# The head of a fused attention and gated-FFN kernel in another order: two engines share its copies, and later loads change places

## The chip, the cores and the metric

One core of a Trainium2 chip runs one kernel. Its engines work at the same time, each through its own list of instructions in order: TensorE (PE in the profile; its weight loads are PEld), VectorE (DVE), ScalarE (ACT), GpSimd (POOL) and SyncE (SP). They wait for one another by semaphores. Data comes from the chip's memory by DMA, issued by an engine into a queue and moved by 16 DMA engines. The metric is the device time of one execution in microseconds; less is better. A verdict is faster or slower when the times differ by more than 2%.

## The reference

Eight batches, eight heads of 64. `x` has 512 rows per batch and head, `state` 32. Each reads the other by attention with a softmax; the two results are put one below the other (544 tokens per batch, 512 wide) and go through a gated feed-forward net of inner width 1536.

```python
scores  = scale * x @ state.T;   a  = softmax(scores);  xread = a  @ state     # (8, 8, 512, 64)
scores2 = scale * state @ x.T;   a2 = softmax(scores2); sread = a2 @ x         # (8, 8,  32, 64)
t = concatenate([xread, sread], axis=2)   # heads side by side: 4608 tokens x 512
gate = 1 / (1 + exp(-(t @ w_gate)));  val = t @ w_val                          # 512 -> 1536
out  = (gate * val) @ w_out                                                    # 1536 -> 512
```

## The kernel before

**What is computed per batch b.** `xT_mm`, `xT_cp`: x transposed by TensorE into PSUM and copied out (batches 0 and 1; later ones are transposed by a DMA that SyncE issues, `at_xT_dma`, L140). `S_mm`, `S_exp` (L147 to L167; for batch 0 in four pieces `Sq_mm`, `Sq_exp`, L174, L182): scores and their exponential E. `n_sum` (L208, L210; in pieces `nq_sum`, L186, L188): row sums and reciprocals on VectorE. `n_mul` (L227; `nq_mul`, L193): the normalised weights. `aT_mm`, `aT_cp` (L234, L244) or `aT_dma` (L248): these transposed. `at_Eb` (L200): four casts of E for the state's read, `rd_mm`, `rd_fin` (L265 to L275).

**The state is multiplied into the net's weights first.** `sw_visit(b, lo, n, ...)` (L286, L293) multiplies the state of batch b with columns lo to lo+n of both weights, head by head; `sw_cp` (L329) copies the result from PSUM to `SW`, in two halves e. So the attention's read and the first layer are one product: `gv_mm(b, f)` (L343) makes the gate and the value of the f-th 128 of the 1536 columns from `SW` and aT in four matmuls of 512 columns. `gv_th` (L364) is the tanh on ScalarE (the sigmoid is made of it), `gv_glu` (L369) the product on VectorE.

**The second layer** is a product of 2x2 blocks done with seven block products instead of eight. `ht_sum(t)` (L400) makes differences of blocks of `w_out` into T, `h_sum(t, half)` (L407) sums of blocks of the gated values into Sm; `h_mm(k, c)` (L442) is product k of batch 0, for one of two groups of rows; `w_keep` and `w_add` (L430, L433) put the products together, `w_store` sends the rows out.

**Loads.** `load_w(w, lo, n)` (L104) loads columns of the gate (w=0) or value (w=1) weights, `load_wo(q)` (L107) a third of `w_out`, `load_xh` and `load_x(2)` (L100, L82) x of batches 1 and 2, `load_sb(q)` (L527) the states of batches 2q and 2q+1. GpSimd issues all of these, one after the other among its other work, into one software queue (q0); they cast to bf16 where the target is bf16. `load_xp` is issued by SyncE, in hardware queue q1.

**What sets the order.** Nothing is reordered by a scheduler: each call emits its instructions at once, and each engine runs its own in the order of the calls in the source. Eight PSUM banks of one 128x512 tile each are named by hand (G0, G1, OU, S0 to S3, AT); a call that puts a new tile into a bank waits until the old one was read. The head, L560 to L838, is one list of calls written by hand that interleaves batch 0, batch 1 and the beginning of batch 2. Behind it stands a loop `step(b, f)` from b = 2 on, whose gate and value products are L355 and whose output products are L425.

Of the kernel before, what the change touches and what calls it, by code (L numbers as in the profile page):

```python
# [16 lines left out]
def kernel(  # L17
# [75 lines left out]
    def cast_xp(b, cp, lo, n):  # L93
        xh_tile(b)
        cp(xhs[b][:, lo:lo + n], xfs[b][:, lo:lo + n])

    def load_xh(b, lo, n):
        xh_tile(b)
        v = x[b].rearrange("h (p c) d -> p h c d", c=4)
        nc.gpsimd.dma_start(xhs[b][:, lo:lo + n], v[:, lo:lo + n])  # L100
# [9 lines left out]
    def zero(t, eng):  # L110
        (nc.gpsimd if eng is pool else nc.vector).memset(t, 0.0)
# [22 lines left out]
    def xT_cp(b, j, cp, n=1):  # L134
        cp(xT_tile(b)[:, j:j + n], held["xT", b, j])
# [192 lines left out]
    def sw_cp(b, lo, w, e, cp):  # L328
        cp(*sw_left.pop((b, lo, w, e)))  # L329
# [242 lines left out]
    cast_s(0, vec)
    cast_xp(0, act, 0, 2)
    load_xh(1, 4, 4)
    zero(sTd, vec)
    sT_mm(0, S1)
    load_xp(0, nc.sync, 4, 2)
    cast_xp(0, vec, 4, 2)
    xT_mm(0, 0, G1)
    load_xp(0, nc.sync, 2, 2)  # L580
    cast_xp(0, vec, 2, 2)
    xT_mm(0, 2, OU)
    xT_cp(0, 0, vec)
    xT_mm(0, 1, S3)
    sT_pad(0, act)
    sT_pad(1, act)
    xT_cp(0, 2, act)
    load_xp(0, nc.sync, 6, 2)
    cast_xp(0, act, 6, 2)
    Sq_mm(0, 2, S1)  # L590
# [24 lines left out]
    nq_mul(0, 0, pool)
    xT_mm(1, 2, S1, 2)
    nq_mul(0, 2, vec)
    nq_mul(0, 1, pool)
    xT_cp(1, 2, vec, 2)
    S_mm(1, 0, OU)  # L620
    S_exp(1, 0)
    load_w(1, 1280, 256)
# [1 line left out]
    at_Eb(0)
    aT_mm(0, AT)
    aT_cp(0, 0, act)
    S_mm(1, 1, S2)
    load_w(0, 1280, 256)
    aT_cp(0, 1, act)
    sw_visit(0, 256, 256, G0, G1)  # L630
    sw_cp(0, 256, 2, 0, vec)
# [26 lines left out]
    gv_mm(0, 2, S2, S1)
    gv_th(0, 2)
    gv_glu(0, 2)  # L660
    gv_mm(0, 9, AT, S3)
    gv_mm(1, 3, G1, S0)
# [8 lines left out]
    sT_mm(2, S1)
    gv_mm(1, 8, S2, S3)
    zero(sTz, pool)
    gv_th(1, 8)
# [25 lines left out]
    gv_mm(0, 10, G1, S3)  # L700
    sw_visit(0, 512, 512, OU, AT, 0)
    gv_glu(0, 8)
    gv_th(0, 10)
# [1 line left out]
    gv_glu(0, 0)
    gv_glu(0, 10)
    sw_cp(0, 512, 0, 0, act)
    gv_mm(0, 11, S2, G1)
    sw_visit(1, 512, 512, S3, S1, 0)
    sw_visit(0, 512, 512, OU, S0, 1)  # L710
    sw_cp(0, 512, 0, 1, vec)
    gv_th(0, 11)
    sw_visit(1, 512, 512, AT, G0, 1)
    sw_cp(1, 512, 0, 0, act)
    sw_cp(0, 512, 1, 1, act)
    gv_glu(0, 11)
    load_wo(1)
    sw_cp(0, 512, 1, 0, vec)
    rd_mm(1, S2)
    sw_cp(1, 512, 0, 1, act)  # L720
    gv_mm(0, 5, G1, OU)
    rd_fin(1)
    gv_th(0, 5)
    gv_mm(0, 7, S1, S3)
    sw_cp(1, 512, 1, 0, vec)
    sw_cp(1, 512, 1, 1, act)
    gv_glu(0, 5)
    nc.gpsimd.memset(xs[:, :, :, D:], 1.0)
    gv_mm(0, 4, S0, G0)
    gv_th(0, 7)  # L730
    gv_glu(0, 7)
    gv_th(0, 4)
    gv_glu(0, 4)
    gv_mm(0, 6, S1, G1)
    cast_x(2, pool, 4, 4)
    load_wo(2)
    gv_th(0, 6)
    sw_wide(2, 1, S3, OU, S0, G0, S2, AT)
    gv_glu(0, 6)
    sw_cp(2, 1, 0, 1, act)  # L740
# [6 lines left out]
    sw_cp(2, 1, 2, 0, act)
    h_sum(0, 1, vec)
    gv_mm(1, 6, OU, S3)
    sw_visit(1, 1280, 256, S1, G0)  # L750
# [4 lines left out]
    h_sum(2, 0, pool)
    h_sum(2, 1, vec)
    sw_cp(1, 1280, 2, 1, act)
    gv_mm(1, 4, G1, OU)
    gv_glu(1, 6)
    cast_x(2, pool, 0, 4)  # L760
    gv_mm(1, 7, S1, AT)
    gv_th(1, 4)
    sw_cp(1, 0, 2, 1, vec)
# [9 lines left out]
    h_mm(1, 0, AT)
    h_mm(1, 1)
    ht_sum(0, vec)
    h_sum(0, 0, pool)
    h_mm(5, 0, G1)
    S_mm(2, 0, OU)
    h_mm(5, 1)
    ht_sum(2, vec)  # L780
    h_sum(1, 0, vec)
    load_x(3, nc.sync)
    ht_sum(1, vec)
# [3 lines left out]
    sw_cp(1, 0, 2, 0, act)
    h_sum(3, 0, pool)
    w_keep('V1', 1)
    h_mm(6, 0)  # L790
    S_exp(2, 0)
    n_sum(2, 0)
    n_mul(2, 0, pool)
    S_mm(2, 1, G0)
    aT_dma(2, 0)
    S_exp(2, 1)
    gv_mm(1, 0, OU, S2)
    h_sum(3, 1, vec)
# [238 lines left out]
```

## Time and profile before

| | |
|---|---|
| time, median of 3 runs (lowest to highest) | 212.96 us (212.92 to 215.22) |
| profiled execution: time | 213.24 us |
| profiled execution: span | 211.5 us |
| instructions in the span | 5331 |
| mean granted TensorE clock | 0.992 |
| DMA packets, MB | 40920, 27.14 |

The span runs from the first to the last instruction that the profiler saw; 1.74 us of the execution lie around it. In the timelines a row gives the start and the length in us, the engine, the line and operation, what it writes and reads, how many instructions are taken together, and in brackets the idle time before them and who ended it. In the table of stretches the columns are PE, PEld, DVE, ACT and POOL busy time with their counts, then the granted clock, the DMA share and GB/s.

### The profile page before, as it was taken

The numbers are of one execution on the slowest core, as the hardware profiler recorded it, in microseconds if no ns is written. First come the engines' busy times: TensorE is split into PE (matmuls) and PEld (weight loads), VectorE is DVE, ScalarE is ACT, GpSimd is POOL, SyncE is SP. The second block draws the span as 40 slices with busy tenths as digits, with TensorE's granted clock in tenths as the row PEclk, the third lists the DMA queues.
The fourth block names the chain that finished last, engine by engine and source line by source line (L and its number), as shares of the span: only waits on it lengthen the run. The fifth ranks groups of instructions, "written<-read, shape, count | busy, mean of one in ns | idle before, by whom it ended". The sixth has DMA issues, their size and how long they took to land.

```text
span 211.5 us, 5331 instructions
## 1 busy us (share of the span) xinstructions
PE 204.5 (97%) x2089; PEld 133.4 (63%) x2089; DVE 160.7 (76%) x308; ACT 129.6 (61%) x244; POOL 78.7 (37%) x104
## 2 busy tenths in 40 slices
PE   7789999999999999999999999999999999999992
PEld 2555443677666666565656565657566666788982
DVE  2698899998987788578876887687848876864682
ACT  3878898754767477855786578647774673233210
POOL 8899467599042705900391029301500000000010
PEclk9799999999999999999999999999999999999999
DMA  6999999761689943985924621264110500130044
GB/s 190 181 192 192 213 289 192 115 215 38 78 219 342 132 94 133 289 73 160 295 58 48 186 87 28 56 101 175 26 34 1 201 2 0 76 126 0 4 171 126
DMA packets 40920, 27.14 MB, mean 128 GB/s; under 512 B 23616, under 2 KB 38720, under 8 KB 40896
## 3 DMA queue, kind: packets, MB, share of 16 engines
q1 hardware_dynamic: 30544, 19.47, 36.9%
q0 software_dynamic: 9920, 7.01, 20.5%
q10 hardware_dynamic: 432, 0.33, 0.7%
q8 instruction: 16, 0.26, 0.5%
q14 instruction: 8, 0.07, 0.1%
HBM read 18.35 MB, written 8.91 MB: 129 GB/s over the span
## 4 chain that ended last, share of the span: by engine, by line
PE 94%; DMA 2%; DVE 1%; ACT 1%; SPq 0%; issue 0%
PE gvp L355 30%; PE outp L425 29%; PE gvp L343 10%; PE gvp L358 5%; PE outp L442 4%; PE swp L286 4%; PE swp L293 2%; PE outp L484 2%; DMA xf<-in_x_dram 2%; PE Sp L147 1%; PE xTp L132 1%; PE outp L467 1%; PE rdp L262 1%; PE warm L517 1%; PE aTp L234 1%; PE rdp L265 1%
## 5 line engine op out<-in xcount | busy, mean ns | idle before, releaser
L369 DVE SCALAR_TENSOR_TENSOR glu<-th,gvp 128x512 bf16<-128x512 f32 (+1 forms) x108 | 70.1, 654 | 36.7 <-PE gvp L355 13.7
L364 ACT ACTIVATE th<-gvp 128x512 f32<-128x512 f32 (+1 forms) x108 | 62.1, 578 | 49.4 <-PE gvp L355 34.8
L355 PE MATMUL gvp<-aT,SW 128*128 128x512 bf16 x288 | 77.5, 380 | 0.1
L329 ACT CAST SW<-swp 128x512 bf16<-128x512 f32 x83 | 46.6, 594 | 9.2 <-PE swp L286 8.3
L425 PEld LDWEIGHTS <-Sm 128*128 128x128 bf16 x324 | 31.7, 98 | 12.6
L355 PEld LDWEIGHTS <-SW 128*128 128x128 bf16 x288 | 26.6, 98 | 17.3 <-issue 3.6
L200 POOL CAST Eb<-E 128x256 bf16<-128x256 f32 x32 | 12.8, 436 | 52.0 <-ACT E L167 52.0
L425 PE MATMUL outp<-tw,Sm 128*128 128x256 bf16 x240 | 31.8, 273 | 0.0
L425 PEld LDWEIGHTS <-glu 128*128 128x128 bf16 x240 | 23.5, 98 | 10.2
L425 PE MATMUL outp<-wo,glu 128*128 128x256 bf16 x168 | 22.9, 273 | 0.0
L343 PE MATMUL gvp<-aT,SW 128*128 128x512 bf16 x96 | 22.6, 380 | 0.0
L509 POOL DMA_DIRECT2D out_dram<-res x1 | 0.6, 612 | 50.3 <-DVE res L433 50.3
L227 POOL TENSOR_TENSOR ab<-E,ri 128x512 bf16<-128x512 f32 x13 | 14.3, 1101 | 11.7 <-DVE ri L210 7.0
L407 DVE TENSOR_TENSOR Sm<-glu 128x768 bf16<-128x768 bf16 (+1 forms) x34 | 18.0, 535 | 0.0
L433 DVE SCALAR_TENSOR_TENSOR res<-outp,U 128x512 f32<-128x512 f32 x22 | 15.0, 685 | 1.2 <-PE outp L442 0.9
L343 PEld LDWEIGHTS <-SW 128*128 128x128 bf16 x96 | 8.7, 98 | 10.5 <-issue 1.9
L116 POOL CAST xb<-xf 128x1024 bf16<-128x1024 f32 x12 | 13.2, 1127 | 1.6 <-DMA xf<-in_x_dram 1.6
L167 ACT ACTIVATE E<-Sp 128x512 f32<-128x512 f32 x14 | 8.4, 599 | 7.1 <-PE Sp L147 5.7
L358 PE MATMUL gvp<-xb,wgv 128*128 128x256 bf16 x96 | 12.6, 273 | 0.0
L425 PE MATMUL outp<-wo,Sm 128*128 128x256 bf16 x84 | 11.5, 273 | 0.0
L358 PEld LDWEIGHTS <-wgv 128*128 128x128 bf16 x96 | 9.3, 98 | 1.4
L251 POOL CAST xs<-xf 128x1024 bf16<-128x1024 f32 x10 | 10.1, 1040 | 0.0
(106 smaller groups left out, 224.9 us busy)
## 6 DMA issues: line engine op xcount, KB each, us to landing
out_dram<-res SPq DMA_DIRECT2D x14, 512.0 KB, 3.2
xf<-in_x_dram SPq DMA_DIRECT2D x5, 1024.0 KB, 7.5
wo<-in_moe_w_out_dram POOLq DMA_DIRECT2D x3, 512.0 KB, 8.2
xf<-in_x_dram SPq DMA_DIRECT2D x4, 256.0 KB, 4.0
wgv<-in_moe_w_gate_dram POOLq DMA_DIRECT2D x4, 256.0 KB, 7.4
wgv<-in_moe_w_val_dram POOLq DMA_DIRECT2D x4, 256.0 KB, 8.8
xf<-in_x_dram POOLq DMA_DIRECT2D x1, 1024.0 KB, 9.2
xf<-in_x_dram POOLq DMA_DIRECT2D x2, 256.0 KB, 6.2
```

What stands on the lines that cost most here:

```text
L116: cp(xbs[b].rearrange("p c h d -> p h c d")[:, lo:lo + n], (xhs if b in xhs else xfs)[b][:, lo:lo + n])
L200: nc.gpsimd.tensor_copy(Ebs[b][:, c], E1s[b][:, c])
L227: (nc.gpsimd if eng is pool else nc.vector).tensor_tensor(half(b, i, abs_), e1, ri.unsqueeze(len(ri.shape)).to_broadcast(e1.shape), ALU.mult)
L329: cp(*sw_left.pop((b, lo, w, e)))
L343: nc.tensor.matmul(ps, SWs[b][:, g, w, fs], aTs[b][:, :, g], start=(g == 0), stop=(g == 1))
L355: nc.tensor.matmul(ps, SWs[b][:, g, w, fs], aTs[b][:, :, g], start=(g == 0), stop=(g == 1))
L358: nc.tensor.matmul(ps, (wg, wv)[w][:, j, fs], held["XS"][:, j], start=(j == 0), stop=(j == 3))
L364: nc.scalar.activation(th, held["gv", b, f][0], AF.Tanh, scale=0.5)
L369: nc.vector.scalar_tensor_tensor(glus[b][:, f], held["th", b, f], 1.0, held["gv", b, f][1], ALU.add, ALU.mult)
L407: eng.tensor_tensor(S_(b, t)[:, i], a, c, op)
L425: nc.tensor.matmul(wps[key][:, c], lhs[:, i, c * 128:(c + 1) * 128], rhs[:, i], start=(first and c == 0 and i == 0), stop=(i == NF // 2 - ...
L433: nc.vector.scalar_tensor_tensor(to, wps[key], 0.5, held["w", name], ALU.mult, ALU.add)
```

## The change

The list of calls of the head is written in another order; the loop and all helpers stay. The calls are nearly the same ones: some copies and casts go to another engine, tiles go to other PSUM banks. The matmuls are the same in number and shape. Where engines change: of the copies of batch 0's x and of its aT, VectorE now makes some that ScalarE made, and the other way round, among them half of aT (`aT_cp(0, 0, vec)`) and half of the padded state (`sT_pad(1, vec)`); `n_mul(1, 1)` goes from VectorE to GpSimd; `h_sum(1, 1)` and `h_sum(0, 0)` go from GpSimd to VectorE. The states of later batches are loaded behind the first eight weight loads. The diff, cut:

```diff
-    load_sb(2)
...
-    load_w(0, 0, 256)
     load_sb(1)
-    sw_visit(1, 256, 256, OU, S3)
+    gv_mm(0, 3, S0, AT)
     sw_cp(1, 256, 2, 0, act)
-    load_sb(3)
-    gv_mm(0, 3, G0, S1)
-    n_mul(1, 1, vec)
+    gv_th(0, 2)
+    gv_glu(0, 2)
+    sw_visit(0, 1024, 256, OU, S1)
+    n_mul(1, 1, pool)
     gv_th(0, 3)
     load_w(0, 512, 512)
-    sw_visit(0, 1024, 256, G1, AT)
-    sw_cp(1, 256, 2, 1, act)
-    sw_visit(1, 1024, 256, OU, G0)
-    sw_cp(0, 1024, 2, 1, act)
-    load_w(1, 512, 512)
...
+    at_Eb(1)
+    rd_mm(1, S2)
+    load_sb(3)
+    load_w(1, 512, 512)
...
+    h_mm(1, 0, AT)
+    h_mm(2, 0, G0)
+    h_sum(0, 0, vec)
+    gv_th(1, 4)
+    ht_sum(0, vec)
+    ht_sum(2, vec)
...
-    gv_mm(1, 11, S3, G1)
-    h_sum(1, 1, pool)
+    h_mm(7, 0, S0)
+    h_mm(7, 1)
+    gv_mm(1, 0, S2, G0)
```

**Three places.** GpSimd, from the casts of batch 0 (`Eb`) to the loads of `w_out`: 128x4x512 is the last third of the gate or value weights, `in_state` a load of later states. Before:

```order
L200 CAST Eb<-E_177 128x256 x4
L104 DMA wgv<-in_moe_w_gate_dram 128x4x256
L227 TENSOR_TENSOR ab<-E_265,ri 128x8x64
L104 DMA wgv<-in_moe_w_gate_dram 128x4x256
L527 DMA tw<-in_state_dram 128x4x64 x2
L104 DMA wgv<-in_moe_w_gate_dram 128x4x512
L104 DMA wgv<-in_moe_w_val_dram 128x4x512
L200 CAST Eb<-E_265 128x256 x4
L111 MEMSET sTz 128x2048
L82 DMA xf<-in_x_dram 128x8x256
L107 DMA wo<-in_moe_w_out_dram 128x4x512
```

And in the changed kernel:

```order
L200 CAST Eb<-E_168 128x256 x4
L527 DMA tw<-in_state_dram 128x4x64
L227 TENSOR_TENSOR ab<-E_267,ri 128x8x64
L527 DMA tw<-in_state_dram 128x4x64
L227 TENSOR_TENSOR ab<-E_267,ri 128x8x64
L104 DMA wgv<-in_moe_w_gate_dram 128x4x512
L111 MEMSET sTz 128x2048
L200 CAST Eb<-E_267 128x256 x4
L527 DMA tw<-in_state_dram 128x4x64
L104 DMA wgv<-in_moe_w_val_dram 128x4x512
L82 DMA xf<-in_x_dram 128x8x256
L107 DMA wo<-in_moe_w_out_dram 128x4x512 x3
```

The last value load stood right behind the last gate load; now the memset, four casts and a state load stand between them. A second multiplication of batch 1 stands ahead of the gate load, and the three loads of `w_out` follow one another.

VectorE, ahead of its first copy of a state-times-weight product (L329). Before:

```order
L193 TENSOR_TENSOR ab<-E_177,riq 128x8x32 x2
L135 COPY xT<-xTp 128x1024
L208 TENSOR_REDUCE rs<-E_265 128x16
L210 RECIPROCAL ri<-rs 128x16
L329 CAST SW<-swp 128x2x256
```

And in the changed kernel:

```order
L193 TENSOR_TENSOR ab<-E_168,riq 128x8x32 x2
L135 COPY xT<-xTp 128x1024
L244 COPY aT<-aTp 128x512
L208 TENSOR_REDUCE rs<-E_267 128x16
L210 RECIPROCAL ri<-rs 128x16
L329 CAST SW<-swp 128x2x256
```

Half of the copy of batch 0's aT, which ScalarE made, is new in this row.

VectorE, from the first difference of blocks of `w_out` (L400) to the second add that frees an output product's bank for good. Before:

```order
L400 TENSOR_TENSOR tw<-wo 128x1536 x2
L407 TENSOR_TENSOR Sm<-Sm,glu 128x768
L400 TENSOR_TENSOR tw<-wo,tw 128x1536
L369 SCALAR_TENSOR_TENSOR glu<-th,gvp 128x512
L208 TENSOR_REDUCE rs<-E_911 128x16
L210 RECIPROCAL ri<-rs 128x16
L407 TENSOR_TENSOR Sm<-glu,Sm 128x768
L208 TENSOR_REDUCE rs<-E_911 128x16
L210 RECIPROCAL ri<-rs 128x16
L400 TENSOR_TENSOR tw<-wo,tw 128x1536
L433 SCALAR_TENSOR_TENSOR U_957<-outp,U_947 128x512
L369 SCALAR_TENSOR_TENSOR glu<-th,gvp 128x512 x2
```

And in the changed kernel, up to the four gates and the add behind them:

```order
L407 TENSOR_TENSOR Sm<-glu 128x768
L407 TENSOR_TENSOR Sm<-Sm,glu 128x768
L400 TENSOR_TENSOR tw<-wo,tw 128x1536
L208 TENSOR_REDUCE rs<-E_884 128x16
L210 RECIPROCAL ri<-rs 128x16
L369 SCALAR_TENSOR_TENSOR glu<-th,gvp 128x512
L433 SCALAR_TENSOR_TENSOR res<-outp,V_875 128x2x256
L369 SCALAR_TENSOR_TENSOR glu<-th,gvp 128x512
L433 SCALAR_TENSOR_TENSOR U_946<-outp,U_944 128x512
L407 TENSOR_TENSOR Sm<-glu,Sm 128x768
L400 TENSOR_TENSOR tw<-wo,tw 128x1536
L208 TENSOR_REDUCE rs<-E_884 128x16
```

Ahead of these the changed kernel has the first two differences (`x2`) and one sum; behind them a reciprocal, four gates in a row and the adds. So six gates stand behind the first difference where three stood, and two sums more.

More of the change, by code (lines that the diff above doesn't have):

```diff
@@ L570 @@
     load_xh(1, 0, 4)
-    nc.vector.memset(ones, 1.0)
[L572 to L590, printed above, removed]
@@ L615 @@
[L615 to L622, printed above, removed]
-    n_sum(1, 0)
[L624 to L631, printed above, removed]
-    S_exp(1, 1)
+    zero(sTd, vec)
+    cast_s(0, vec)
+    load_xh(1, 4, 4)
+    cast_xp(0, vec, 0, 2)
+    sT_mm(0, G1)
@@ new lines @@
+    load_xp(0, nc.sync, 4, 2)
+    load_xp(0, nc.sync, 2, 2)
+    cast_xp(0, vec, 4, 2)
+    load_w(0, 256, 256)
+    sT_pad(0, act)
+    xT_mm(0, 0, S0)
+    xT_mm(0, 2, OU)
+    xT_cp(0, 0, act)
+    sT_pad(1, vec)
+    Sq_mm(0, 0, S1)
+    Sq_exp(0, 0)
+    load_w(1, 256, 256)
+    load_w(1, 1024, 256)
+    xT_cp(0, 2, vec)
+    Sq_mm(0, 2, S3)
+    load_w(0, 1024, 256)
+    nq_sum(0, 0)
+    load_xp(0, nc.sync, 6, 2)
+    warm(3, S1)
+    Sq_exp(0, 2)
+    cast_xp(0, act, 2, 2)
+    xT_mm(0, 1, S3)
@@ new lines @@
+    nq_sum(0, 2)
+    nq_mul(0, 0, pool)
+    cast_xp(0, vec, 6, 2)
+    xT_cp(0, 1, vec)
+    xT_mm(0, 3, S1)
+    load_w(1, 1280, 256)
+    xT_cp(0, 3, vec)
+    Sq_mm(0, 1, G1)
+    Sq_mm(0, 3, S2)
+    Sq_exp(0, 1)
+    load_w(1, 0, 256)
+    nq_mul(0, 2, pool)
+    xT_mm(1, 0, G1, 2)
+    nc.vector.memset(ones, 1.0)
+    xT_mm(1, 2, S1, 2)
+    Sq_exp(0, 3)
+    nq_sum(0, 1)
+    nq_sum(0, 3)
+    xT_cp(1, 0, act, 2)
+    nq_mul(0, 1, vec)
+    nq_mul(0, 3, vec)
+    xT_cp(1, 2, vec, 2)
+    S_mm(1, 0, S2)
@@ L633 @@
+    load_w(0, 0, 256)
+    load_w(0, 1280, 256)
+    S_exp(1, 0)
+    aT_mm(0, OU)
+    S_mm(1, 1, AT)
+    aT_cp(0, 1, act)
+    sw_visit(0, 256, 256, S1, G0)
+    aT_cp(0, 0, vec)
+    at_Eb(0)
+    load_sb(2)
+    n_sum(1, 0)
+    S_exp(1, 1)
+    n_mul(1, 0, pool)
+    sw_visit(1, 256, 256, S3, S2)
+    sw_cp(0, 256, 2, 0, act)
+    sw_cp(0, 256, 2, 1, vec)
+    rd_mm(0, G1)
     n_sum(1, 1)
-    rd_mm(0, AT)
-    sw_cp(0, 256, 2, 1, act)
-    n_mul(1, 0, pool)
     rd_fin(0)
-    load_w(0, 0, 256)
+    gv_mm(0, 2, OU, G0)
@@ L654 @@
+    aT_mm(1, S2)
+    zero(sTz, pool)
+    sw_cp(0, 1024, 2, 1, vec)
     sw_cp(1, 1024, 2, 0, act)
-    aT_mm(1, S0)
+    gv_mm(0, 8, S3, OU)
     gv_glu(0, 3)
     aT_cp(1, None, vec)
[L658 to L662, printed above, removed]
+    sw_cp(1, 1024, 2, 1, act)
+    gv_th(0, 8)
+    gv_glu(0, 8)
+    gv_mm(0, 9, G0, S1)
     gv_th(0, 9)
-    sw_cp(1, 1024, 2, 1, vec)
-    gv_mm(1, 2, AT, G0)
+    gv_mm(1, 9, AT, S3)
+    gv_mm(1, 8, S0, G1)
@@ L666 @@
     gv_glu(0, 9)
+    gv_th(1, 9)
+    gv_mm(1, 3, OU, G0)
+    gv_th(1, 8)
     gv_th(1, 3)
+    gv_glu(1, 9)
+    gv_glu(1, 8)
+    sw_visit(0, 0, 256, S1, S0)
+    sw_visit(0, 1280, 256, S2, AT)
+    sw_cp(0, 0, 2, 0, act)
     gv_glu(1, 3)
-    nc.scalar.activation(pre[:, 0:1], ones, AF.Exp)
+    gv_mm(1, 2, OU, G1)
+    sT_mm(2, S3)
+    sw_cp(0, 1280, 2, 0, act)
     gv_th(1, 2)
[L671 to L674, printed above, removed]
+    sw_cp(0, 0, 2, 1, vec)
     gv_glu(1, 2)
-    load_x(2, nc.gpsimd)
@@ L700 @@
[L700 to L703, printed above, removed]
-    pad(2, 6)
[L705 to L740, printed above, removed]
@@ L741 @@
-    sw_cp(2, 1, 0, 0, vec)
-    sw_cp(2, 1, 1, 1, vec)
-    sw_cp(2, 1, 1, 0, act)
+    sT_cp(2, vec)
+    sT_mm(1, S1)
+    gv_mm(0, 1, S2, G0)
+    gv_th(0, 1)
+    gv_mm(0, 0, S0, OU)
+    sw_visit(0, 512, 512, S3, G1, 0)
+    at_Eb(1)
+    rd_mm(1, S2)
+    load_sb(3)
+    load_w(1, 512, 512)
+    gv_th(0, 0)
+    sw_cp(0, 1280, 2, 1, act)
+    sT_cp(1, vec)
+    load_x(2, nc.gpsimd)
+    gv_glu(0, 0)
+    sw_cp(0, 512, 0, 1, act)
+    load_wo(2)
+    gv_mm(0, 10, S0, S1)
+    rd_fin(1)
+    sw_cp(0, 512, 0, 0, act)
@@ new lines @@
+    gv_th(0, 10)
+    gv_mm(0, 11, S2, OU)
+    gv_glu(0, 1)
+    sT_mm(3, G0)
+    gv_th(0, 11)
+    gv_glu(0, 10)
+    gv_glu(0, 11)
+    sw_visit(0, 512, 512, AT, S0, 1)
+    sw_visit(1, 512, 512, S1, S2, 0)
+    sT_cp(3, act)
+    sw_visit(1, 512, 512, G1, S3, 1)
+    sw_cp(0, 512, 1, 0, act)
+    sw_cp(1, 512, 0, 0, act)
+    sw_cp(0, 512, 1, 1, vec)
+    sw_cp(1, 512, 0, 1, vec)
+    gv_mm(0, 7, G0, OU)
+    gv_mm(0, 5, S0, S1)
+    gv_th(0, 7)
+    gv_th(0, 5)
+    gv_mm(0, 4, S2, AT)
+    sw_cp(1, 512, 1, 0, vec)
@@ L744 @@
+    load_wo(0)
+    gv_th(0, 4)
+    load_wo(1)
+    cast_x(2, pool, 4, 4)
+    sw_cp(1, 512, 1, 1, act)
+    gv_glu(0, 7)
+    gv_glu(0, 5)
+    gv_mm(0, 6, S0, G1)
+    gv_glu(0, 4)
+    gv_th(0, 6)
+    gv_glu(0, 6)
+    sw_wide(2, 1, OU, S2, G0, AT, S0, S3)
+    sw_cp(2, 1, 0, 1, vec)
+    sw_cp(2, 1, 1, 0, vec)
+    sw_cp(2, 1, 0, 0, act)
+    pad(2, 6)
+    sw_cp(2, 1, 1, 1, act)
     gv_mm(1, 5, S1, G1)
+    gv_mm(1, 6, OU, S2)
     gv_th(1, 5)
+    sw_cp(2, 1, 2, 0, act)
+    cast_x(2, pool, 0, 4)
@@ L746 @@
+    sw_visit(1, 0, 256, AT, G0)
+    sw_visit(1, 1280, 256, S0, S1)
     gv_glu(1, 5)
[L747 to L750, printed above, removed]
     gv_th(1, 6)
     sw_cp(2, 1, 2, 1, act)
-    sw_visit(1, 0, 256, S2, S0)
-    sw_cp(1, 1280, 2, 0, act)
[L755 to L763, printed above, removed]
@@ L764 @@
-    gv_glu(1, 4)
-    gv_th(1, 7)
-    gv_glu(1, 7)
-    gv_mm(1, 11, S3, G1)
-    h_sum(1, 1, pool)
+    gv_glu(1, 6)
+    at_xT_dma(2)
+    h_sum(2, 0, pool)
+    sw_cp(1, 1280, 2, 1, act)
+    gv_mm(1, 7, G1, OU)
+    h_sum(0, 1, vec)
+    gv_mm(1, 4, S2, S1)
+    sw_cp(1, 0, 2, 0, act)
+    sw_cp(1, 0, 2, 1, act)
+    h_mm(1, 0, AT)
[4 more added lines that the diff above has]
+    ht_sum(2, vec)
+    S_mm(2, 0, S2)
+    h_mm(1, 1)
+    gv_th(1, 7)
+    h_mm(2, 1)
@@ new lines @@
+    h_mm(5, 0, G1)
+    h_sum(1, 1, vec)
+    h_sum(2, 1, vec)
+    w_keep('V1', 1)
+    h_sum(1, 0, vec)
+    h_mm(5, 1)
+    S_exp(2, 0)
+    h_sum(3, 0, pool)
+    S_mm(2, 1, S3)
+    ht_sum(1, vec)
+    nc.gpsimd.memset(xs[:, :, :, D:], 1.0)
+    load_x(3, nc.sync)
+    sw_cp(1, 1280, 2, 0, act)
+    h_mm(6, 0)
+    n_sum(2, 0)
+    h_mm(6, 1)
+    gv_glu(1, 7)
+    nc.scalar.activation(pre[:, 0:1], ones, AF.Exp)
+    w_add(2, 'V1', w_res(0, 0)[:, :, lo_])
+    gv_glu(1, 4)
+    h_mm(7, 0, S0)
@@ L769 @@
+    h_mm(7, 1)
+    gv_mm(1, 0, S2, G0)
+    n_mul(2, 0, pool)
+    S_exp(2, 1)
+    w_keep('U2', 1)
+    h_U4()
+    h_sum(3, 1, vec)
+    aT_dma(2, 0)
+    gv_mm(1, 1, OU, S3)
+    gv_th(1, 0)
+    ht_sum(3, vec)
+    gv_th(1, 1)
+    n_sum(2, 1)
+    gv_mm(1, 11, AT, S2)
+    cast_x(3, pool, 4, 4)
     gv_th(1, 11)
-    at_xT_dma(2)
-    gv_mm(1, 10, G0, S1)
+    gv_mm(1, 10, S1, OU)
+    gv_glu(1, 1)
     gv_glu(1, 11)
[L773 to L783, printed above, removed]
     gv_th(1, 10)
-    h_mm(7, 0, S0)
+    h_mm(3, 0)
+    h_mm(3, 1)
+    gv_glu(1, 0)
+    n_mul(2, 1, pool)
     gv_glu(1, 10)
[L787 to L798, printed above, removed]
@@ L822 @@
-    sw_cp(2, 0, 1, 1, act)
-    sw_cp(2, 0, 0, 1, act)
-    sw_cp(2, 0, 2, 0, act)
+    cast_x(3, pool, 0, 4)
+    sw_wide(2, 0, S3, AT, S1, S2, OU, G0)
+    aT_dma(2, 1)
+    sw_cp(2, 0, 0, 1, act)
+    sw_cp(2, 0, 1, 1, act)
+    sw_cp(2, 0, 2, 0, act)
+    w_add(7, 'U4', w_res(0, 1)[:, :, hi_])
+    at_xT_dma(3)
     w_add(5, 'U2', w_res(0, 0)[:, :, hi_])
```

69 lines of the change are left out of this document (2 added, 67 removed).

## The prediction

> **What bounds the kernel now.** I read the shares first, then the chain that ended last, then the timelines of the three engines and the queue on which that chain could come to wait. From the page:
>
> ```profile
> PE 204.5 (97%) x2089; PEld 133.4 (63%) x2089; DVE 160.7 (76%) x308; ACT 129.6 (61%) x244; POOL 78.7 (37%) x104
> ...
> PE 94%; DMA 2%; DVE 1%; ACT 1%; SPq 0%; issue 0%
> ```
>
> TensorE is busy for 97% of the span and makes 94% of the chain. The chain inside the stretch that the change touches:
>
> ```profile
> 14.83 0.97 PE gvp L343 x4
> ...
> 36.36 3.60 PE gvp L343 x16
> 39.96 1.96 PE outp L442 x18
> ...
> 50.79 1.42 PE outp L442 x12
> ...
> 53.65 0.97 PE gvp L355 x4
> ```
>
> Each piece begins where the one before it ends: from 14.83 us, the first gate/value product, to 53.65, where the loop over batches starts with the first product of batch 2, TensorE has no gap. TensorE's instructions are the same in number and kind in both kernels. So the change can gain nothing in that stretch by hiding waits; it can gain or lose only by when the stretch begins and by new waits inside it. What follows 53.65 is bound by TensorE too and is not edited, so a shift there is carried to the end. **I forecast the time at which the loop starts, against 53.65.**
>
> **Part 1, the start.** In the old order VectorE copies half of the first state-times-weight result (L329) at 13.61, and ScalarE the other:
>
> ```profile
> 6.76 0.41 DVE L135 COPY xT<-xTp 128x512 bf16<-128x512 bf16 x1
> ...
> 12.57 0.69 DVE L208 TENSOR_REDUCE rs<-E 128x16 f32<-128x512 f32 x1
> 13.29 0.25 DVE L210 RECIPROCAL ri<-rs 128x16 f32<-128x16 f32 x1
> 13.61 0.69 DVE L329 CAST SW<-swp 128x512 bf16<-128x512 f32 x1
> ```
>
> ```profile
> 12.66 1.07 ACT L244 COPY aT<-aTp 128x512 bf16<-128x512 bf16 x2
> ...
> 14.11 0.61 ACT L329 CAST SW<-swp 128x512 bf16<-128x512 f32 x1
> ```
>
> ScalarE's copy ends last, at 14.72. In the new order VectorE has, just ahead of its copy, half of the copy of aT, which waits until ScalarE's half is through, and the row sum and reciprocal of batch 1. ScalarE's pair ends at 13.73 in this trace; its half is about as late in the new order, and I take 14.05 for the exponential that now stands ahead. Then half an aT (a 128x512 bf16 copy) 0.41, sum and reciprocal about 0.9, the copy 0.69: 16.0. The first product then ends at 16.7 against 15.80, 0.9 late. One visit of the next weights (8 matmuls, some 0.3) that used to come behind it is then already done, so TensorE enters the stretch about **0.55 us late**; 0 if ScalarE is through half a us earlier, 1 if VectorE's added casts push it. This term counts only if nothing later is worse.
>
> **Part 2, the weights.** All weight, state and some x loads are issued by GpSimd, in its program's order:
>
> ```profile
> 2.73 1.65 POOL L100 DMA_DIRECT2D xf<-in_x_dram  x2
> ...
> 13.86 1.06 POOL L227 TENSOR_TENSOR ab<-E,ri 128x512 bf16<-128x512 f32 x1
> ...
> 15.66 1.47 POOL L527 DMA_DIRECT2D tw<-in_state_dram  x2
> 17.12 0.77 POOL L104 DMA_DIRECT2D wgv<-in_moe_w_gate_dram  x1
> 17.85 0.79 POOL L104 DMA_DIRECT2D wgv<-in_moe_w_val_dram  x1
> 18.59 1.46 POOL L200 CAST Eb<-E 128x256 bf16<-128x256 f32 x4
> 19.96 1.84 POOL L111 MEMSET sTz<- 128x2048 bf16 x1
> ...
> 31.93 0.74 POOL L107 DMA_DIRECT2D wo<-in_moe_w_out_dram  x1
> ```
>
> Now the last gate load (L104, 512 columns) is followed by the 1.84 us memset, the 1.46 us of casts and a state load; only then comes the last value load. A multiplication of 1.06 us (L227) is also moved here from VectorE and stands ahead of the gate load. It needs the reciprocal of batch 1's second half, which VectorE gives at about 16.9 by part 1; a state load is issued meanwhile, the multiplication ends at 18.3, the gate load's issue at 19.0, the memset at 20.8, the casts at 22.2, the third state load at 22.95. The value load is issued at 22.95, not 17.85.
>
> Does the queue run dry? Its record, first in the 0.1 us in which its first packets appear, then from 5 to 23.5 us:
>
> ```profile
> q0 software_dynamic: 3, 0.00, 11.9%
> ```
>
> ```profile
> q0 software_dynamic: 7305, 3.27, 138.3%
> ```
>
> The queue kept its engines taken throughout (a share over 100% is packets that overlap). Up to and including the gate load the new order puts 3.28 MB into it: ten loads of 0.262 MB, two states of 0.066, one load of 0.524. At the old rate these 3.27 MB have moved by 23.5. The first load of all was issued at 2.73 and the first packets of the queue show between 5.4 and 5.5: **2.7 us from issue to first packet**. With that delay the third state load (issued at 22.2) brings data from 24.9 and the value load from 25.6, so of 2.1 us only some 0.35 are used, for the state: **1.7 us lost**. Its bounds are 0, if the delay is short once the queue runs, and 1.75, the whole gap with only the state in it. The remaining bytes are those of before, so the landing of the last output weights moves by the same:
>
> ```profile
> wo<-in_moe_w_out_dram POOLq DMA_DIRECT2D x1, 512.0 KB, 7.0
> ```
>
> Issued at 31.93 and landed 7.0 later, at 38.95; now about **40.7** (0 to 0.5 more if the transposes of batch 2 lie on it longer). The first eight loads are not late: the last of them lands near 21 and its first user stands after 22.8.
>
> [...]
>
> **Part 3, the waits on the output weights.** The first output product (L442) needs all three output loads. It stood behind 22 gate/value products and now stands behind 20; two of these take 1.8 (3.60 for 16 matmuls, four products), so TensorE comes there at 39.96 − 1.8 + 0.55 = 38.7 and waits until 40.7, two us in which it has nothing. The differences of output weights on VectorE (L400) wait for the same loads, and behind them stands everything up to the last add that releases the second-last product. The same run of instructions in the old order, VectorE:
>
> ```profile
> 38.19 1.88 DVE L369 SCALAR_TENSOR_TENSOR glu<-th,gvp 128x512 bf16<-128x512 f32 x3
> 39.99 1.82 DVE L400 TENSOR_TENSOR tw<-wo 128x1536 bf16<-128x1536 bf16 x2
> 41.72 0.55 DVE L407 TENSOR_TENSOR Sm<-Sm,glu 128x768 bf16<-128x768 bf16 x1
> 42.19 0.95 DVE L400 TENSOR_TENSOR tw<-wo,tw 128x1536 bf16<-128x1536 bf16 x1
> ...
> 43.66 0.68 DVE L208 TENSOR_REDUCE rs<-E 128x16 f32<-128x512 f32 x1
> 44.37 0.25 DVE L210 RECIPROCAL ri<-rs 128x16 f32<-128x16 f32 x1
> ...
> 46.73 0.68 DVE L433 SCALAR_TENSOR_TENSOR U<-outp,U 128x512 f32<-128x512 f32 x1
> ...
> 49.40 1.35 DVE L433 SCALAR_TENSOR_TENSOR res<-outp,U 128x512 f32<-128x512 f32 x2 [0.20 <-PE outp L442]
> ```
>
> Start to start, a difference takes 0.87, a sum of glu halves (L407) 0.48, a row sum with its reciprocal 0.88, a gate (L369) or an add (L433) 0.6. Behind the landing T the new order has: four differences 3.48, four sums 1.93, two row sums 1.76, two adds and two gates 2.4, which make 9.57; then gates of (1,1) and (1,11), 1.2; the tanh of (1,10) on ScalarE waits for the second of them, because its product takes the bank that this gate frees, and the gates after it and the add end at T + 12.8. In the old order the sum (1,1) among these ran on GpSimd, and the sum (2,1) and the gates of (1,4), (1,7) and (1,11) were done before the landing. Behind the add stand what stood behind it before, 53.65 − 50.79 = 2.86: the last product, the state read of batch 2 and its weights. So the loop starts at T + 12.88 + 2.86 = T + 15.74. TensorE alone needs less: 53.65 − 39.96 and two products 1.8, about 15.4, less the 0.2 of two matmuls that can run earlier. **VectorE binds, by half a us.** With T = 40.7 the loop starts at 56.45, 2.8 us late. The 0.55 of part 1 and the earlier arrival of TensorE lie inside its wait and cost nothing more; if T were early they would be what is next.
>
> **Sum.** The profiled execution took 213.24, of which 211.5 is the span and 1.74 lies around it. 213.24 + 2.8 = 216.04; it stood 0.28 over the median of 212.96, so 215.8 on the median's scale, 1.3% slower.
>
> **The rivals.**
>
> *The queue doesn't run dry* (0.22). [...] For it: the old trace never shows the queue in want of an order, so the 2.7 is the delay of an idle queue only. Against: the order itself is 5 us later.
>
> *Not slower* (0.13). The last output load ends early. Of its queue only this is left from 37.5 to 38.7, while the transposes that SyncE issued run on the same engines:
>
> ```profile
> q0 software_dynamic: 41, 0.04, 18.6%
> ```
>
> ```profile
> 35.99 5.20 SPq L140 DMA_TRANSPOSE xT<-xb  x4
> ```
>
> 41 packets trail by 1.2 us. The three output loads are now issued back to back, and the transposes wait for two casts and a pad behind them; if the loads are through before the transposes begin, T is 37.5 to 37.9. The point from which it decides is T = 53.65 − 15.74 = 37.9, and VectorE has to be ready then as well, 0.7 earlier than I walk it. Price −0.4 to 0: 212.8.
>
> *The clock drops* (0.10). TensorE's wait of two us at the first output product comes with a price of its own. Early in this trace it waited:
>
> ```profile
> 6.90 0.40 PE L132 MATMUL xTp<-ident,xf 128*128 128x128 bf16 x4 [1.08 <-DVE xf L95]
> ```
>
> and the granted clock (the third value from the end) then was
>
> ```profile
> 7.50:8.00 0.50, 0.23 (x7) 0.19 (x6) 0.26 (x1) 0.50 (x3) 0.50 (x1) 0.88 1.17 149
> 8.00:8.50 0.50, 0.50 (x8) 0.35 (x5) 0.38 (x1) 0.36 (x2) 0.50 (x2) 0.50 1.30 163
> ...
> 11.00:11.50 0.50, 0.50 (x9) 0.50 (x7) 0.50 (x2) 0.09 (x1) 0.50 (x1) 0.70 1.45 197
> ```
>
> half for some 3.4 us, from 7.9 to 11.3. The same again costs 1.7 of TensorE's time, of which VectorE's lead hides up to half a us: 217.0 to 217.5, more if it lasts for two such stretches. [...]
>
> **How the numbers follow.** The forecast has 0.50, with a range of its own of 215.2 to 216.3 (1.2 us lost to 0.5 more at the transposes). The remaining 0.05 is for things not seen. Reaching from the not-slower case to the lower end of the clock's leaves about 0.15 out: 212.4 to 217.1. Two per cent, 4.3 us, is about what a measurement of this kernel can tell from no change: below 208.7 lies no case, only 0.02 of the unseen; above 217.2 half of the clock's case and most of the unseen, 0.09; the rest, 0.89, lies within.
>
> **What would show it.** The changed profile should have the value load issued near 23 and a stretch of one to two us near 24 to 25.6 in which the software queue carries little; the last output load landing near 40.7; an idle time of about two us on TensorE ahead of L442, released by that DMA; VectorE without idle time from there to the add ahead of the second-last output product; TensorE's wait for that add; L355 first at about 56.5 and equal spacing behind. If the queue shows no thin stretch, part 2 is wrong; if the add isn't what releases the last product, part 3. The forecast fails altogether if the first gate/value product begins a us earlier than now and no wait shows at L442.

## The result, and the profile after

The changed kernel takes 215.68 us (median of 15 runs, 214.86 to 216.87) against 213.13 of the kernel before in the same runs: ratio 1.0104, 95% interval 1.0077 to 1.0131. It is slower by about 1%, within the two per cent. The profiled execution took 216.03 with a span of 214.2, against 213.24 and 211.5. One execution further down, the first profile of experiment 1, ran at a granted clock of 0.756 and took 267.72 us; the ratios leave such executions out.

The shares and the chain of the changed kernel:

```profile
PE 204.5 (95%) x2089; PEld 132.7 (62%) x2089; DVE 162.4 (76%) x312; ACT 128.6 (60%) x241; POOL 75.7 (35%) x103
...
PE 76%; DVE 9%; DMA 7%; POOL 4%; issue 1%; ACT 1%; DVEq 0%; POOLq 0%
```

TensorE works as long as before, 204.5, but holds only 76% of the chain, not 94%. The pieces that took its place (start, length, what):

```profile
18.88 1.82 POOL sTz L111
...
25.82 14.64 DMA wo<-in_moe_w_out_dram
...
40.75 1.83 DVE tw L400 x2
...
48.14 1.13 DVE Sm L407
...
53.42 0.61 DVE res L433
54.03 0.04 issue
54.08 1.47 PE outp L442 x12
...
56.95 0.97 PE gvp L355 x4
```

The chain goes through the memset on GpSimd, the output loads, and VectorE's run from the first differences to the add. The loop starts at 56.95 instead of 53.65, 3.3 us late; the span is 2.7 longer. From there to the end it is 157.25 here (214.2 − 56.95) and was 157.85 (211.5 − 53.65): about half of the 0.6 is regained inside the loop, half behind the last add (L473). The half inside the loop is no scatter. From the loop's start to the last add it is 153.79 in the kernel before and in experiment 6, which keeps the old order, and 153.52 to 153.54 in the changed kernel and in all experiments on it but the eighth. Where it comes from stays open.

GpSimd issued the loads nearly when the prediction had them:

```profile
18.08 0.80 POOL L104 DMA_DIRECT2D wgv<-in_moe_w_gate_dram  x1
18.88 1.82 POOL L111 MEMSET sTz<- 128x2048 bf16 x1
20.62 1.42 POOL L200 CAST Eb<-E 128x256 bf16<-128x256 f32 x4
22.00 0.74 POOL L527 DMA_DIRECT2D tw<-in_state_dram  x1
22.73 0.77 POOL L104 DMA_DIRECT2D wgv<-in_moe_w_val_dram  x1
```

The software queue between 23.5 and 26 us (packets, MB, share), before and then after:

```profile
q0 software_dynamic: 509, 0.51, 122.2%
```

```profile
q0 software_dynamic: 704, 0.24, 108.2%
```

It moved 0.24 MB where it had moved 0.51. What is missing, 0.27 MB at the old rate of 0.2 MB per us, is 1.3 us. TensorE waited for the value load itself at its first use (L286), and then at the first output product; VectorE waited at the first differences:

```profile
30.17 0.84 PE L286 MATMUL swp<-wgv,tw 64*32 64x512 bf16 x24 [0.36 <-DMA wgv<-in_moe_w_val_dram]
...
39.41 0.38 PE L442 MATMUL outp<-wo,glu 128*128 128x256 bf16 x2
40.51 1.25 PE L442 MATMUL outp<-wo,glu 128*128 128x256 bf16 x10 [0.72 <-DMA wo<-in_moe_w_out_dram]
```

```profile
40.75 1.83 DVE L400 TENSOR_TENSOR tw<-wo 128x1536 bf16<-128x1536 bf16 x2 [1.41 <-DMA wo<-in_moe_w_out_dram]
...
48.06 1.21 DVE L407 TENSOR_TENSOR Sm<-glu,Sm 128x768 bf16<-128x768 bf16 x1
```

The last output load landed near 40.47 (25.82 + 14.64, both rounded). One row wasn't expected: the sum at 48.06 took 1.21 where its like took 0.55. GpSimd was then casting:

```profile
47.82 1.04 POOL L116 CAST xb<-xf 128x1024 bf16<-128x1024 f32 x1 [0.38 <-DMA xf<-in_x_dram]
```

### The profile page after: what moved, and what is told of

The parts are those of the page before. It is cut to its first block, busy times and chain, and to the rows that moved or that the text cites. A ratio compares the mean times of both kernels' runs of the same rounds, so it can differ in the third digit from the quotient of the medians.

```text
span 214.2 us, 5324 instructions
## 1 busy us (share of the span) xinstructions
PE 204.5 (95%) x2089; PEld 132.7 (62%) x2089; DVE 162.4 (76%) x312; ACT 128.6 (60%) x241; POOL 75.7 (35%) x103
## 4 chain that ended last, share of the span: by engine, by line
PE 76%; DVE 9%; DMA 7%; POOL 4%; issue 1%; ACT 1%; DVEq 0%; POOLq 0%
PE gvp L355 30%; PE outp L425 29%; DMA wo<-in_moe_w_out_dram 7%; PE gvp L358 5%; PE swp L286 3%; PE outp L484 2%; PE warm L517 2%; DVE tw L400 2%; DVE glu L369 2%; DVE Sm L407 1%; PE Sp L147 1%; PE outp L467 1%; PE swp L293 1%; POOL ab L227 1%; POOL sTz L111 1%
## 5 line engine op out<-in xcount | busy, mean ns | idle before, releaser
L355 PE MATMUL gvp<-aT,SW 128*128 128x512 bf16 x288 | 77.4, 379 | 0.0
L329 ACT CAST SW<-swp 128x512 bf16<-128x512 f32 x85 | 47.5, 593 | 6.9 <-PE swp L286 6.1
L355 PEld LDWEIGHTS <-SW 128*128 128x128 bf16 x288 | 26.7, 98 | 17.2 <-issue 3.0
L425 PEld LDWEIGHTS <-glu 128*128 128x128 bf16 x240 | 23.5, 98 | 10.2
L407 DVE TENSOR_TENSOR Sm<-glu 128x768 bf16<-128x768 bf16 (+1 forms) x35 | 18.7, 540 | 0.0
L116 POOL CAST xb<-xf 128x1024 bf16<-128x1024 f32 x12 | 13.3, 1130 | 6.9 <-ACT th L364 6.4
L251 POOL CAST xs<-xf 128x1024 bf16<-128x1024 f32 x10 | 10.1, 1041 | 0.0
```

The costliest lines, as they stand in the source:

```text
L116: cp(xbs[b].rearrange("p c h d -> p h c d")[:, lo:lo + n], (xhs if b in xhs else xfs)[b][:, lo:lo + n])
L355: nc.tensor.matmul(ps, SWs[b][:, g, w, fs], aTs[b][:, :, g], start=(g == 0), stop=(g == 1))
L407: eng.tensor_tensor(S_(b, t)[:, i], a, c, op)
L425: nc.tensor.matmul(wps[key][:, c], lhs[:, i, c * 128:(c + 1) * 128], rhs[:, i], start=(first and c == 0 and i == 0), stop=(i == NF // 2 - ...
```

## The experiments

Loop starts below are the first L355 in the chain of that run's profile (56.95 in the changed kernel, 53.65 before). Each is from one profiled execution, which can stand up to 0.8 us from the median of its kernel (experiment 6: 213.80 against 214.63). Times are medians, and ratios are against the kernel before.

**1. The last value load early.**

```diff
     load_w(0, 512, 512)
+    load_w(1, 512, 512)
     sw_cp(0, 1024, 2, 0, act)
...
     load_sb(3)
-    load_w(1, 512, 512)
```

> The changed kernel with the last value load put back right behind the last gate load, ahead of the memset and the casts. Theory (the software queue ran dry for lack of this order, and the end of the output loads moved by that): the load is issued near 18.9, no thin stretch in the queue near 24 to 26 us, last output load landed near 39.0 instead of 40.47, the differences (L400) begin near 39.1, the loop starts 1.4 to 1.7 us earlier than in the changed kernel (near 55.4 against 56.95), time near 214.1. Rival (the landing is set by the packets that trail among the transposes, or the queue is served at the same rate anyway): landing and loop start within 0.4 us of the changed kernel, time near 215.7.

Time 214.5, ratio 1.0063 (1.0040 to 1.0086). The lines below are from a second profile of this kernel, a single execution of 215.02:

> The first experiment once more for a profile at full clock: the last value load right behind the last gate load. As there: issued near 18.9, no thin stretch in the queue, last output load landed near 39.0, loop start near 55.4; rival: landing within 0.4 of 40.47.

The queue from 23.5 to 26, VectorE and the chain there:

```profile
q0 software_dynamic: 609, 0.51, 127.7%
```

```profile
39.53 1.83 DVE L400 TENSOR_TENSOR tw<-wo 128x1536 bf16<-128x1536 bf16 x2 [0.67 <-DMA wo<-in_moe_w_out_dram]
```

```profile
55.91 0.97 PE gvp L355 x4
```

The thin stretch is gone, the differences begin 1.22 earlier and the loop 1.04 earlier. So the late order did move the landing. The other profiles agree: with the late value load (changed kernel, experiments 2, 4 and 5) the last output load landed between 40.0 and 40.5, with the early one (1, 3, 7, 8 and 9) between 38.7 and 39.2. Less came through than expected (1.4 to 1.7): the differences began only 1.22 earlier, and a difference now ran beside the GpSimd cast and lost 0.84 (1.79 us instead of 0.95), where the changed kernel lost 0.66 with a sum.

**2. Three sums ahead of the differences.**

```diff
+    h_sum(1, 1, vec)
+    h_sum(2, 1, vec)
+    h_sum(1, 0, vec)
     ht_sum(0, vec)
     ht_sum(2, vec)
```

(with the three lines taken out below)

> The changed kernel with three sums of glu halves (L407) put ahead of the first two differences (L400), into the 1.4 us in which VectorE waited for the output loads. Theory (VectorE's run behind the landing sets when the loop starts): the run behind the landing is 1.4 us shorter, or 2.1 if the sum that took 1.21 us now meets no GpSimd instruction; then TensorE's own work behind the landing (15.2 us by the prediction) binds, so the loop starts 1.2 to 1.4 us earlier, near 55.7, time near 214.4. Rival (something else sets it: TensorE's work or the transposes of aT): no change beyond 0.3 us.

Time 216.08, ratio 1.0132 (1.0095 to 1.0169): no gain. VectorE's differences, GpSimd beside them, and the loop:

```profile
40.33 3.27 DVE L400 TENSOR_TENSOR tw<-wo 128x1536 bf16<-128x1536 bf16 x2
```

```profile
40.36 2.42 POOL L407 TENSOR_TENSOR Sm<-glu,Sm 128x768 bf16<-128x768 bf16 x1 [2.51 <-DVE Sm L407]
```

```profile
56.67 0.97 PE gvp L355 x4
```

The two differences took 3.27, not 1.83: the 1.44 that was taken out of the run came back in it. The third moved sum is what GpSimd's sum waits for, so that now started with the differences. The loop starts 0.28 earlier, which is the rival's number, but not for the rival's reason.

**3. Both edits.**

> The changed kernel with both edits: the early value load and the three sums ahead of the differences. Theory: the landing at 39.0 comes while VectorE still makes the sums (to about 40.5), so VectorE gains only what the second edit gives and 0.3; TensorE's work from 39.0 allows 54.2. The loop starts near 54.5, 2.4 us earlier than in the changed kernel, less than the sum of both alone; time near 213.3. Rival (the two are independent terms and add up): 2.8 or more earlier, 54.1 or less, time near 212.8. Rival (only one of them matters): 1.2 to 1.6 earlier.

Ratio 1.0064 (1.0040 to 1.0089), time 214.65, loop start 55.38. The last rival came nearest, 1.57 earlier, for the reason of the second run: the two differences again took 3.27, from 39.73, with GpSimd's sum from 39.90. Whether the terms add up could not be read from it.

**4. The start.**

```diff
-    sw_cp(0, 256, 2, 1, vec)
+    sw_cp(0, 256, 2, 1, act)
```

> The changed kernel with the half of the first state-times-weight copy that VectorE made (L329, 15.03 us) given to ScalarE, which makes it second of its row of such copies. Theory (the later start of the first products is swallowed by the wait for the output loads): the second half of the first product starts near 15.3 instead of 15.71, TensorE waits about 0.4 longer ahead of L442 for it, the loop starts within 0.15 us of the changed kernel. Rival (the late start is carried to the end): the loop starts 0.4 us earlier, time 0.4 lower.

Ratio 1.0105 (1.0078 to 1.0131), time 215.67: no change of the time, as expected, but the gain was lost at another place than was named. TensorE, first the row of the changed kernel, then those of this run:

```profile
15.71 1.69 PE L343 MATMUL gvp<-aT,SW 128*128 128x512 bf16 x7 [0.52 <-DVE SW L329]
```

```profile
14.91 2.17 PE L343 MATMUL gvp<-aT,SW 128*128 128x512 bf16 x8 [0.15 <-ACT SW L329]
17.02 0.76 PE L293 MATMUL swp<-wgv,tw 64*32 64x512 bf16 x16
18.31 0.62 PE L234 MATMUL aTp<-ident,ab 128*128 128x128 bf16 x8 [0.53 <-POOL ab L227]
```

The first products run through without their wait of 0.52, and at 18.3 TensorE waits 0.53 for the multiplication that the change gave to GpSimd. The changed kernel begins the same transposes at 18.20. So the earlier start is swallowed here already: TensorE comes to L442 at 39.09, as in experiments 2 and 5, which do not have this edit. The loop start, 56.59, is 0.36 earlier, outside the expected 0.15 and next to the rival's 0.4. But 0.28 of it is that the differences began at 40.47 in this run, and they did so in experiment 5 too; the rest is that the sum beside the cast took 1.13 instead of 1.21.

**5. The GpSimd cast to ScalarE.**

```diff
     gv_th(1, 0)
+    cast_x(3, act, 4, 4)
...
-    cast_x(3, pool, 4, 4)
```

> The changed kernel with one cast of batch 3's x (L116, 47.82 us) given from GpSimd to ScalarE, behind the tanh of (1,0). In the changed kernel the sum on VectorE that began at 48.06, inside this cast, took 1.21 us where its like take 0.55, and in the run with three sums ahead two differences beside a GpSimd sum took 3.27 instead of 1.83. Theory (a bf16 sum of VectorE that starts while GpSimd computes waits until that is through, and VectorE's run sets the loop's start): the sum takes 0.55 to 0.62, the last product (L442) starts 0.5 to 0.7 earlier after the first difference than the 13.33 us of the changed kernel, the loop starts 0.5 to 0.7 earlier, time near 215.0. Rival (that sum is slow for a reason of its own): it takes 1.1 to 1.3 again, no change.

Ratio 1.0084 (1.0061 to 1.0107), time 215.09, against 215.68. VectorE's first difference and the sum, TensorE's last product, and the loop:

```profile
40.47 1.83 DVE L400 TENSOR_TENSOR tw<-wo 128x1536 bf16<-128x1536 bf16 x2 [1.60 <-DMA wo<-in_moe_w_out_dram]
...
47.78 0.55 DVE L407 TENSOR_TENSOR Sm<-glu,Sm 128x768 bf16<-128x768 bf16 x1
```

```profile
53.13 1.47 PE L442 MATMUL outp<-tw,glu 128*128 128x256 bf16 x12 [0.17 <-DVE res L433]
```

```profile
56.01 0.97 PE gvp L355 x4
```

The sum takes 0.55, the last product starts 12.66 behind the first difference (53.13 − 40.47) instead of 13.33 (54.08 − 40.75). That the sum beside the cast was long because of it (1.21 against 0.55) is shown by this, and that VectorE's run set the loop's start; the times alone would not show it, since the intervals of the two ratios overlap. Of the 0.94 by which the loop starts earlier, 0.28 belongs to the earlier beginning.

**6. One part of the change alone, in the kernel before.**

```diff
     load_w(0, 512, 512)
...
-    load_w(1, 512, 512)
...
     zero(sTz, pool)
+    zero(sTz, pool)
+    load_w(1, 512, 512)
```

> The kernel before with one part of the change alone: the last value load behind the casts and the memset, and a second memset added so that it is issued as late as in the changed kernel, near 22.9 us. Theory (the late order empties the queue and delays all that is behind it): a thin stretch near 24 to 25.6, last output load landed near 40.5 instead of 38.95, and TensorE waits 1.7 to 2.0 us for the value weights at their first use (L286, 28.3), which stands earlier here than in the changed order; the loop starts 1.7 to 2.0 us later than 53.65, time near 215. Rival (the issue alone hurts nothing, the queue keeps its rate): landing within 0.4 of 38.95, loop start within 0.4, time near 213.1.

Time 214.63, ratio 1.0037 (1.0011 to 1.0063), loop start 54.22. The queue moved 0.14 MB from 23.5 to 26, less still than in the changed kernel. From 24 to 24.5, from 24.75 to 25, and from 26 to 26.5:

```profile
q0 software_dynamic: 15, 0.01, 14.6%
```

```profile
q0 software_dynamic: 19, 0.02, 157.1%
```

```profile
q0 software_dynamic: 85, 0.09, 112.0%
```

The value load was issued at 23.34. The queue is down to 3 packets in the quarter of a us before 24.75, carries more from there, 1.4 us after the issue, and is back at the full rate at 26, 2.7 us after it. Yet TensorE shows no wait at L286 or L442 in this profile. It was late by 0.53 before the edited loads are used at all (22.96 against 22.43 at the same matmuls, behind a value load that both kernels issue at 6.55 and that landed 9.7 us later here), by 0.53 at L286 and by 0.54 at L442:

```profile
22.96 0.56 PE swp L293 x16
...
28.85 0.77 PE swp L286 x24
...
40.50 1.98 PE outp L442 x18
...
54.22 0.97 PE gvp L355 x4
```

In this execution my expectation failed: the value load landed 5.6 us after its issue, at 28.94, just in time, and the last output load 7.4 after 32.93, at 40.33, just when TensorE came for it. So here, in the old order, the late load itself cost next to nothing; the new order comes to L442 two products earlier and waits for it. But the profiled execution, 213.8, is one of the shorter ones. Seven of the twelve took 214.6 to 214.8, 1.3 to 1.5 us more than the median of the kernel before (213.29 in the same runs) and near the 215 that I expected, and the ratio is above 1. Whether those executions waited for the late load, and so what it costs in the old order, stays open.

**7. The early load, and only two sums ahead.**

```diff
     load_w(0, 512, 512)
+    load_w(1, 512, 512)
...
+    h_sum(1, 1, vec)
+    h_sum(2, 1, vec)
     ht_sum(0, vec)
     ht_sum(2, vec)
...
     h_sum(1, 0, vec)
```

> The early value load as in the first experiment, and only two of the three sums ahead of the differences; the third, which GpSimd's sum (L407) waits for, stays behind them, so GpSimd's sum starts when the differences are through. Theory (the gain of the three sums was lost where the differences ran beside GpSimd's sum): the first two differences take 1.83 instead of 3.27 and begin near 39.3; the loop starts 1.2 to 1.4 us earlier than with both edits of the third experiment, near 54.1, time near 213.2, level with the kernel before. Rival (the differences were slow because the landing output loads or something else held them): they take over 3 us again and the loop starts near 55.4.

Time 214.36, ratio 1.0034 (1.0009 to 1.0058). VectorE and GpSimd:

```profile
40.06 1.82 DVE L400 TENSOR_TENSOR tw<-wo 128x1536 bf16<-128x1536 bf16 x2
...
47.04 1.79 DVE L400 TENSOR_TENSOR tw<-wo,tw 128x1536 bf16<-128x1536 bf16 x1
```

```profile
46.76 1.25 POOL L116 CAST xb<-xf 128x1024 bf16<-128x1024 f32 x1 [0.95 <-DMA xf<-in_x_dram]
```

The first two differences are back at 1.82, which settles the second run. The loop starts at 55.65, not 54.1: the fourth difference now meets the cast, 0.84 lost, and the first differences began at 40.06, not at 39.3 (of these 0.76, 0.35 was lost before the first products of TensorE, which began that much later than in the first experiment).

**8. Besides, the cast later and the start of experiment 4.**

```diff
-    cast_x(3, pool, 4, 4)
...
     n_mul(2, 1, pool)
+    cast_x(3, pool, 4, 4)
```

> The two sums ahead of the differences with the early value load, and besides: the half copy given to ScalarE as in the fourth experiment, and the first cast of batch 3's x (L116) put behind GpSimd's second multiplication of batch 2, so that no GpSimd instruction runs beside VectorE's fourth difference, which took 1.79 us beside that cast where its like take 0.95. Theory (with the landing, the waiting behind GpSimd and the run behind the landing gone, TensorE's own work is all that is left): the fourth difference takes 0.95, TensorE has no wait for VectorE ahead of the last product beyond 0.2, the loop starts between 54.4 and 54.9, time 213.2 to 213.8, level with the kernel before. Rival (another wait takes the place, the cast's delay at the casts for the state read above all): the loop starts at 55.3 or later, time 214.2 or more.

TensorE has no gap from 18.8 to the loop; the fourth difference takes 0.95 and the loop starts at 54.6, as expected (TensorE's row, since the chain does not pass through this start):

```profile
54.56 1.04 PE L355 MATMUL gvp<-aT,SW 128*128 128x512 bf16 x4
```

But the time is 214.44, ratio 1.0066 (1.0053 to 1.0079). That is the rival's time: another wait took the place, though not the one that was named. Inside the loop the first sum stands beside GpSimd's next casts, and a gate behind it is late for TensorE:

```profile
54.30 1.23 DVE L407 TENSOR_TENSOR Sm<-glu 128x768 bf16<-128x768 bf16 x1
```

```profile
53.08 2.04 POOL L251 CAST xs<-xf 128x1024 bf16<-128x1024 f32 x2
```

```profile
59.44 0.59 PE L355 MATMUL gvp<-aT,SW 128*128 128x512 bf16 x2 [0.45 <-DVE glu L369]
```

**9. Besides, the multiplication back on VectorE, GpSimd's casts earlier.**

```diff
     n_sum(1, 1)
+    n_mul(1, 1, vec)
...
-    n_mul(1, 1, pool)
...
     S_exp(2, 1)
+    at_Eb(2)
...
-    at_Eb(2)
```

> The last version, in which VectorE's first sum inside the loop took 1.23 us beside GpSimd's casts (L251) and TensorE waited 0.53 at 17.8 for the multiplication (L227) that the change moved to GpSimd; now that multiplication is back on VectorE, and the casts for the state read of batch 2 (L200) stand ahead of GpSimd's second multiplication of batch 2, so that the casts L251 are done earlier. Theory (these two waits are what is left): no wait of TensorE near 18, loop start 54.1 to 54.3, VectorE's first sum in the loop 0.55 to 0.6, time 213.2 to 213.5, level with the kernel before. Rival (the loop's first sum is slow for its own reason, or yet another wait takes the place): loop start as in the last version, 54.6, or the sum above 1 us again; time above 214.

Time 213.46, ratio 1.0003 (0.9990 to 1.0016): level with the kernel before. The chain, and VectorE's first sum in the loop:

```profile
17.02 0.74 PE swp L293 x16
17.77 0.55 PE aTp L234 x8
...
54.30 0.97 PE gvp L355 x4
```

```profile
53.98 0.55 DVE L407 TENSOR_TENSOR Sm<-glu 128x768 bf16<-128x768 bf16 x1
```

With these edits the loss in time is gone. The loop still starts 0.65 later than before (54.30 against 53.65); some 0.25 of that comes back inside the loop, as in the other versions of the new order. The edits were aimed at the late value load, at VectorE's run behind the landing, at its meeting with GpSimd (the versions on the way met it at other places, and the casts moved here meet VectorE too, a sum of 0.68 and a difference of 1.15), and at the start: the half copy on VectorE, for which TensorE waits 0.52 in the changed kernel, and behind it the multiplication on GpSimd. Experiments 7 to 9 change several of these at once, so they do not give a price for each. None of the versions beat the kernel before.

## Why the prediction was right, point by point

*What bounds.* Right: TensorE's work is unchanged (204.5 us busy in both), and the loss is new waits ahead of the loop. That a shift of the loop's start is carried to the end holds but for the 0.3 that the new order regains in the loop.

*Part 1, the start.* VectorE's half copy was at 15.03 to 15.6, not until 16.0, since ScalarE's half of aT ended at 13.78 instead of 14.05 and the sum and reciprocal overlap a little. But what this part made of the multiplication on GpSimd was incomplete: I counted it only for the loads behind it, while TensorE waits for it too. The run without the late half copy (4) lost its gain at this wait, ahead of L442.

*Part 2, the weights.* Right in mechanism and nearly in size. The value load's issue was forecast at 22.95 and came at 22.73; 1.7 us of queue were to be lost, 1.3 were by the bytes; landing 40.7 forecast, 40.47 measured, and 40.0 to 40.2 in the three other profiles with the same order of loads. The first experiment shows the cause. What the sum left out is the first use of the value weights: TensorE waited 0.36 for them at L286. The 2.7 us, read from one row as the delay to the first packet, fits experiment 6 as the delay to the full rate; there the queue moved only 15 packets from 0.7 to 1.2 us after the issue, and more came from 1.4 us after it. The rows do not say which load a packet belongs to. The rival of a queue that doesn't run dry falls by the 0.24 MB where 0.51 had moved.

*Part 3, VectorE's run.* T + 12.88 was forecast for the last product; it came at 54.08, T + 13.6. The term that was too small is the sum of glu halves, 0.48 a piece: one of the four took 1.21. The beginning was 0.28 behind the landing, which the sum had left out. Some 0.2 came back: the four gates ran without the wait for the tanh of (1,10) that I had put among them. TensorE came to L442 at 39.41, not 38.7, 0.36 of it by the wait at L286, and so stood still for 0.7, not two us. That VectorE binds is shown by experiment 5. By how much: in 8, where TensorE has no wait, it needs 15.47 from its first output product to the loop (39.09 to 54.56; about 15.4 was forecast), or 15.25 without the first two matmuls. Behind these two it took 15.7 in 5 (40.23 to 55.95) and 16.4 in the changed kernel (40.51 to 56.88). So without the collision VectorE binds by half a us, as forecast, and with it by 1.1.

*The sum.* Loop start 56.45 forecast, 56.95 measured; 0.6 came back later, which I had put at nothing. So that 215.8 came so near to 215.68 is partly luck: two errors cancel. The difference of the medians, 2.55, is also a little less than the forecast 2.8, since the kernel before has 213.13 over more runs and not 212.96.

*The rivals.* The not-slower case needed a landing by 37.9; even with the early load the differences waited until 39.53. The clock did not drop: in the changed kernel the granted clock is 1.00 from 15 to 54 us, and its mean of 0.997 is above the 0.992 of before. TensorE stood still for 0.7 us only, so no run shows whether a wait of two us would have lowered it.

## What to carry to other kernels

When a load is moved in its engine's program, count all that the engine does between it and the load before it, compare that with how long the queue's stock lasts, and add the delay from issue to data (2.7 us to the first packet of the first load, in the kernel before): here the value load was issued 4.65 us after the gate load (22.73 against 18.08), behind a memset, casts and a state load, and the queue then moved 0.24 MB in a stretch in which it had moved 0.51. The price also hangs on who comes first for the last bytes: in the one profile of experiment 6 TensorE came for the output weights at 40.3, just as they landed, and not at 39.4, and did not wait. And before work is moved into an idle time of VectorE, look at which GpSimd instruction it releases and what VectorE does at that moment.
